# The second dense product of 14 token tiles as exchanged 64-row halves, first loads dealt to other queues, and a new table of steps

## The chip, the cores and the metric

One core of one Trainium2 chip. The metric is the device time of one execution in microseconds (us), as the median of several. The engines are named as the profile does: PE (TensorE matmuls), PEld (its weight loads), DVE (VectorE), ACT (ScalarE), POOL (GpSimd), SP (SyncE, which here only issues transfers). A q behind a name (SPq, ACTq) marks the queue from which a transfer is issued.

## The reference

One attention branch and one dense branch on the same normalized tokens, added to the input. 2048 tokens, width 448, 16 heads of 28, hidden width 1792; inputs and output in bfloat16. There is no gain or bias in the layer norm.

```python
xn = layernorm(x)                                  # over 448, eps 1e-5
q, k, v = split(xn @ wqkv)                         # 16 heads of 28
phi(t) = concat(softmax(t @ w_phi), softmax(-(t @ w_phi)))
kv = sum_s phi(k)_s v_s ;  z = sum_s phi(k)_s      # per head: 56 x 28, 56
o = (phi(q) @ kv) / (phi(q) @ z + 1e-6)
h = xn @ w1 + b1 ;  act = h * tanh(softplus(h))    # 2048 x 1792
out = x + o @ wo + act @ w2
```

## The kernel before

Tokens stand in 16 tiles of 128; two tiles are a unit (u = 0 to 7). A token tile is normalized (`ln_stats`, `ln_rstd`, `ln_apply`), and a unit's two normalized tiles are laid side by side (896 columns) and turned, into 7 chunks of 128 features by 128 tokens (`xnT`): 448 = 3.5 x 128, so the middle chunk holds 64 features of the one tile and 64 of the other. The turning is a transposing transfer of SP (step `xt{u}m`) or, at the start, seven PE transposes and two copies (`xt{u}E`, `xt{u}O`).

Products over 448 features are cut in passes (`passes`). Passes E and O take three chunks at the full height of 128 rows, for the even and the odd tile. Passes A, B and H take 64-row halves: two matmuls at a time, one on rows 0 to 63, one on rows 64 to 127, which write the two banks of a pair of PSUM banks, one for each tile of the unit. A gives the even tile the lower half and the odd tile the upper, B exchanges them, H is the shared middle chunk. So A + B + H = E + O + H. Before a pass A may write its banks, the pass B of the same pair must have ended and the other way round (`pe_pass`).

The query and key weights are first multiplied with w_phi, so that q and k leave PE already as q @ w_phi and k @ w_phi: Wk is turned by PE (`wtk`), Wq comes turned by four transposing transfers (`lqT0` to `lqT3`) and a DVE copy that doubles its last 64 columns (`qd`), and both are multiplied with a block-diagonal w_phi (`wmk`, `wmq`). ACT makes the exponentials of q and k (`exq`, `exk`), DVE the sums and POOL most of the normalizing of k (`kn`). When all eight `kv` steps are done, `kvz` and a transfer lay out kv and z, and per token tile `nd` makes numerators and denominators on PE and six DVE instructions make o, which a transfer turns (`ot`). The first dense product (`f0.*`, `f1.*`: 14 feature chunks for each half of the tokens, as passes A, B, H) ends in one ACT Mish activation per chunk. The second dense product is `g{t}`: for one token tile 14 matmuls of 128 rows by 448 columns. `wo{u}` is the output projection of a unit, as A, B, H, into the same bank as the second dense product of the tile; the last writer is followed by the DVE addition of x (`finish`), then the store.

A bank of a tile gets four parts (`PARTS = 4`: its g and wo A, B, H). The last tile of the order, 15, is written in two pieces (384 and 64 columns).

All instructions stand in the table ORDER: one list of step names. A step appends its instructions to the engines that it uses, so the order of the names is the order on each engine; waits are worked out from what a step reads and writes (`Program`). The ending of a name says who does it: s the SP queue, a ACT, d DVE, p POOL; in load steps it is the queue (`lkma` main rows of Wk on ACT's, `lps` w_phi on SP's). An engine takes its list strictly in order, and a waiting instruction holds all that stands behind it. At the start ACT's queue issues Wk, the tails (last 64 rows) of Wk and Wv, x tiles 4 and 5, 2 and 3, then Wv; SP's issues x tiles 6 and 7, w_phi, the four turned query weights, the rest of x and b1.

Lines of the profile: L300 load of x, L303 main rows of a weight, L308 tails, L312 turned Wq, L329 w_phi, L406 warm-up matmuls on zeros, L441 all passes of q, k, v and the first dense product, L514 PE transposes of tokens, L525 their transfer, L548 transposes of Wk, L572 weight products, L643 kv, L692 transpose of b1, L698 Mish, L721 nd, L790 finish, L825 second dense product, L842 output projection.

Of the kernel before, what the change touches and what calls it, by code (L numbers as in the profile page):

```python
# [12 lines left out]
D = 448  # L13
# [6 lines left out]
FC = F // P  # L20
# [118 lines left out]
class Banks:  # L139
# [44 lines left out]
xn1d q1B v4Aa e6 q1H k6H xt7m xn11d k6A v4Ba kn1.1p v6Ad kn2.0p k6B kn4.1p v6Hd xt0m q6A xt5m q6H l1ms v6Bd q6B k7H k7A k0B kn6.1p k7B k0H
kn1.0p k0A v5Aa kn6.0p v5Ha v7Aa k5A k5H v7Ha v5Ba k5B q4B v7Ba kn0.0p e2 e3 kn4.0p kn0.1p kn2.1p q4A f0.3B e13 e5 e4 q4H f0.2H f0.2A f0.3H
f0.0A f0.3A f0.0H v0Ad e12 kn7.0p kn7.1p v0Hd f0.2B v0Bd f0.0B kn3.1p q5H q5A kn5.1p los kn5.0d kn3.0d q0H q0A q5B kv6 kv4 kv0 kv2 kv1 q0B
f1.7A f1.7H f0.6H f0.6A f1.7B wob f1.12H f1.12A f0.6B f1.12B f0.9A kv5 kv3 kv7 f0.9H e9 kvz f0.13B f0.9B f1.11B f0.13A f1.11A f1.11H f0.10B
f0.13H f0.7B f0.10H f0.10A f1.10B l2.3a f0.12B f0.7A f0.7H f1.10H nd6 e8 f1.10A f0.12A f0.8H f0.12H f0.8A nd7 f1.0B e1 l2.1s e11 e0 f0.8B
f1.0H f1.0A q7B nd2 f1.2H q7A q7H f1.2B f1.8B f1.2A f1.8H f1.1H f1.8A f1.1A f0.11A f0.11H f1.1B l2.0s f1.6B f0.11B f1.6H nd4 f1.6A ot3m
f0.5A f1.9B e15 e10 e14 f0.5B nd5 l2.2s f0.4A f0.5H f1.9A f1.9H f0.4H f1.3A nd1 f1.3H f0.4B f1.5B f1.3B f0.1H nd0 f1.5H f0.1B f1.5A f0.1A  # L190
ot2m ot0m f1.4H f1.4A f1.13B f1.4B wo3A nd3 f1.13A wo3B nd8 wo3H f1.13H ot1m nd11 g6 g2 g7 wo0H nd13 wo0A nd14 wo1B wo0B nd10 wo1A wo1H g0
# [10 lines left out]
def _kernel(es, nc, A_x, A_wqkv, A_w_phi, A_wo, B_w1, B_b1, B_w2, out):  # L202
    def sb(name, shape, dtype):
        return es.enter_context(nc.sbuf_tensor(name, shape, dtype))
# [21 lines left out]
    W2 = sb("W2", [P, FC, D], BF16)  # L226
# [6 lines left out]
    actT = sb("actT", [P, FC, S], BF16)  # L233
# [46 lines left out]
    def bank(b, n=1):  # L280
        return PS[:, b * TCW:(b + n) * TCW]
# [57 lines left out]
    W2P = 4  # L339
# [76 lines left out]
    def pe(fn, r, w, tag, after=()):  # L416
        return op("PE", fn, r=r, w=w, tag=tag, after=after)
# [175 lines left out]
    def xchunk(c, par):  # L593
        return c if c == 3 or par == 0 else 4 + c
# [175 lines left out]
    LAST = int(ORDER.split()[-1][3:])  # L770

    def width(t):
        return CUT if t == LAST else D

    out_bank = {}
    PARTS = 4
    done = {t: 0 for t in range(NT)}

    def out_part(t):

        u = t // 2
        if u not in out_bank:
            out_bank[u] = take2()
        done[t] += 1
        return out_bank[u] + t % 2, done[t] == 1, done[t] == PARTS

    def finish(t):
        b = out_bank[t // 2] + t % 2
        n = width(t)
        op("DVE", lambda e: e.tensor_tensor(x_all[:, t, 0:n], bank(b)[:, 0:n], x_all[:, t, 0:n], ALU.add),  # L790
           r=[pb(b), ("x", t)], w=[("out", t)], tag=f"fin{t}")
        if t == LAST:
            last_columns(t, b ^ 1)
        if done[t] == done[t ^ 1] == PARTS:
            free2(out_bank[t // 2])

    def last_columns(t, b):
        assert done[t ^ 1] == PARTS
# [12 lines left out]
        op("DVE", lambda e: e.tensor_tensor(x_all[:, t, CUT:D], to, x_all[:, t, CUT:D], ALU.add), r=[pb(b), ("x", t)],  # L811
           w=[("outl", t)], tag=f"finl{t}")
# [7 lines left out]
    def ffn2(t):  # L820
        b, first, last = out_part(t)

        def f(e):
            for fc in range(FC):
                ins = e.matmul(bank(b)[:, 0:width(t)], actT[:, fc, tok(t)], W2[:, fc, 0:width(t)],  # L825
                               start=first and fc == 0, stop=last and fc == FC - 1)
# [34 lines left out]
    def add(name, fn, *args):  # L861
        steps[name] = lambda: fn(*args)
# [122 lines left out]
```

## Time and profile before

| | |
|---|---|
| median of 3 runs | 149.89 us (149.85 to 150.07) |
| profiled execution: time / span | 150.82 / 148.9 us |
| PE busy | 143.3 us, 96% |
| DVE, ACT, POOL busy | 101.0, 77.3, 33.2 us |
| granted clock of PE | 1.0 |
| HBM read / written | 7.02 / 1.84 MB |

The span runs from the first to the last instruction of the program; the time holds what lies around it too. A row of the timeline gives the start, the length, the engine, the line, the operation, the tiles as out<-in, rows by columns, and the number of instructions merged. Matmuls overlap, so a row's length is more than the distance to the next row's start; distances from start to start are what PE pays. `64*128` ahead of a shape means a half of 64 rows, `128*128` full height. In the chain of waits each row has its start, its length and who had the work.

### The profile page before, as it was taken

To read this page: it belongs to the slowest core of one execution; us is meant where nothing else is said; L and a number is where in the kernel's file an instruction comes from. 1 tells how busy PE (TensorE), PEld (TensorE's weight loads), DVE (VectorE), ACT (ScalarE), POOL (GpSimd) and SP (SyncE) were. 2 spreads that over 40 slices of the span, in tenths; PEclk is the share of its full clock that TensorE was granted. 3 is DMA by queue.
4 is the path that set the end of the run, shared out by engine and by line. 5 is a ranking of instruction groups with operands and counts; after the bars stand their busy time and mean duration, and the time that the engine had idled before them with its cause. 6 is when DMAs were issued, how large, how long until landed. Compare 5 with 4: busy or idle time off the path is not lost.

```text
span 148.9 us, 3768 instructions
## 1 busy us (share of the span) xinstructions
PE 143.3 (96%) x1628; PEld 74.6 (50%) x1628; DVE 101.0 (68%) x215; ACT 77.3 (52%) x90; POOL 33.2 (22%) x42
## 2 busy tenths in 40 slices
PE   7679999999999999999999999999999999999993
PEld 2355444555556454455444545545555555665552
DVE  0787998999989931089529996989997990042222
ACT  1596999999999986688995774100000000000000
POOL 4002435499999920000000000000000000000000
DMA  4999968999997003997383202200000347000115
GB/s 121 259 198 355 132 160 180 173 236 244 211 171 224 4 4 73 161 292 173 87 188 95 62 4 62 66 0 0 2 4 0 90 95 247 4 0 0 62 66 185
DMA packets 40980, 17.46 MB, mean 117 GB/s; under 512 B 34948, under 2 KB 40196, under 8 KB 40964
## 3 DMA queue, kind: packets, MB, share of 16 engines
q1 hardware_dynamic: 39044, 15.29, 44.6%
q10 hardware_dynamic: 1920, 1.93, 5.8%
q8 instruction: 13, 0.21, 0.7%
q14 instruction: 3, 0.02, 0.0%
HBM read 7.02 MB, written 1.84 MB: 60 GB/s over the span
## 4 chain that ended last, share of the span: by engine, by line
PE 91%; DMA 5%; ACTq 1%; DVE 1%; ACT 0%; issue 0%
PE PS L441 50%; PE PS L825 29%; PE PS L842 7%; DMA Wkv<-in_A_wqkv_dram 5%; PE PS L721 2%; PE PS L643 2%; ACTq L308 1%; PE PS L572 1%; ACTq L300 0%; DVE x_all L790 0%; ACTq L303 0%; ACT L357 0%; DVE x_all L811 0%; PE PS L692 0%
## 5 line engine op out<-in xcount | busy, mean ns | idle before, releaser
L441 PE MATMUL PS<-xnT,W 64*128 64x512 bf16 x392 | 45.0, 376 | 0.0
L825 PE MATMUL PS<-W,actT 128*128 128x448 bf16 (+1 forms) x224 | 42.7, 351 | 0.0
L698 ACT ACTIVATE actT<-PS,b1T 128x1024 bf16<-128x1024 f32 x28 | 29.8, 1114 | 8.7 <-PE PS L441 8.6
L825 PEld LDWEIGHTS PS<-W,actT 128*128 128x128 bf16 x224 | 21.6, 98 | 20.2 <-issue 0.7
L441 PEld LDWEIGHTS PS<-xnT,W 64*128 64x128 bf16 x392 | 18.5, 94 | 20.8 <-ACT actT L698 0.9
L625 POOL TENSOR_TENSOR actT<-actT,rSk 128x896 bf16<-128x896 bf16 x14 | 24.1, 1758 | 2.9 <-DVE rSk L623 2.9
L790 DVE TENSOR_TENSOR x_all<-PS,x_all 128x448 bf16<-128x448 f32 (+1 forms) x16 | 9.5, 616 | 19.7 <-PE PS L825 10.4
L621 DVE TENSOR_REDUCE Sk<-actT 128x32 f32<-128x896 bf16 x16 | 16.7, 1042 | 0.0
L613 ACT ACTIVATE actT<-PS 128x896 bf16<-128x896 f32 x16 | 13.7, 935 | 0.7 <-PE PS L441 0.7
L441 PE MATMUL PS<-Wkv,xnT 64*128 64x448 bf16 (+1 forms) x94 | 13.2, 350 | 0.8 <-DMA Wkv<-in_A_wqkv_dram 0.8
L441 PE MATMUL PS<-Wpq,xnT 64*128 64x448 bf16 (+1 forms) x106 | 13.2, 350 | 0.0
L441 PE MATMUL PS<-Wpk,xnT 64*128 64x448 bf16 (+1 forms) x100 | 12.7, 350 | 0.0
L480 DVE BATCH_NORM_STATS2 stats<-x_all 128x6 f32<-128x448 bf16 x16 | 9.7, 609 | 3.6 <-DMA x_all<-in_A_x_dram 3.6
L737 DVE COPY Sq<-PS 128x32 f32<-128x32 f32 x16 | 2.9, 184 | 13.5 <-PE PS L721 13.5
L746 DVE TENSOR_TENSOR v_all<-v_all 128x464 f32<-128x464 f32 x16 | 10.3, 642 | 0.6
L742 DVE TENSOR_TENSOR v_all<-PS,Sq 128x464 f32<-128x464 f32 x16 | 10.3, 641 | 0.6
L750 DVE TENSOR_TENSOR xn<-v_all,rden 128x448 bf16<-128x448 f32 x16 | 10.0, 624 | 0.6
L744 DVE TENSOR_TENSOR v_all<-PS,Sq 128x464 f32<-128x464 f32 x16 | 10.1, 629 | 0.0
L679 ACT ACTIVATE actT<-PS 128x896 bf16<-128x896 f32 x10 | 8.7, 941 | 0.0
L441 PEld LDWEIGHTS PS<-Wkv,xnT 64*128 64x128 bf16 (+1 forms) x94 | 5.4, 95 | 6.5 <-DMA Wkv<-in_A_wqkv_dram 1.0
L441 PEld LDWEIGHTS PS<-Wpq,xnT 64*128 64x128 bf16 (+1 forms) x106 | 5.4, 94 | 5.2 <-issue 0.4
L441 PEld LDWEIGHTS PS<-Wpk,xnT 64*128 64x128 bf16 (+1 forms) x100 | 5.3, 94 | 4.8 <-issue 0.2
(74 smaller groups left out, 117.1 us busy)
## 6 DMA issues: line engine op xcount, KB each, us to landing
out_dram<-x_all SPq DMA_DIRECT2D x7, 224.0 KB, 2.2
W<-in_B_w_dram SPq DMA_DIRECT2D x1, 1344.0 KB, 7.6
x_all<-in_A_x_dram SPq DMA_DIRECT2D x2, 448.0 KB, 4.6
Wkv<-in_A_wqkv_dram ACTq DMA_DIRECT2D x2, 336.0 KB, 5.8
Wo<-in_A_wo_dram SPq DMA_DIRECT2D x2, 336.0 KB, 3.8
W<-in_B_w_dram SPq DMA_DIRECT2D x2, 336.0 KB, 4.5
x_all<-in_A_x_dram SPq DMA_DIRECT2D x2, 224.0 KB, 3.2
x_all<-in_A_x_dram ACTq DMA_DIRECT2D x2, 224.0 KB, 5.4
```

The source lines that it names most:

```text
L441: ins = e.matmul(o, lhs(c, k), rhs(c, k), start=par in first and n == at[par][0], stop=par in last and n == at[par][-1])
L480: op("DVE", lambda e: e.bn_stats(stats[:, t, :], x_all[:, t, :]), r=[("x", t)], w=[("st", t)], tag=f"bn{t}")
L613: op("ACT", lambda e, s=s: e.activation(E_of(u)[:, s, :, :], two(b, D), ACT.Exp, scale=1.0 if s == 0 else -1.0), r=[pb(b), pb(b + 1)], w=[ ...
L621: op("DVE", lambda e: e.tensor_reduce(Sk[u][:, s, :], Eh(), AX.X, ALU.add), r=[("E", u, s)], w=[("Sk", u, s)], tag=f"Sk{u}.{s}")
L625: op(eng, lambda e: e.tensor_tensor(Eh(), Eh(), ap_on(rSk[u][:, s, 0:1], [[1, 2 * H], [0, DH]]), ALU.mult), r=[("E", u, s), ("rSk", u, s)] ...
L698: op("ACT", lambda e: e.activation(actT[:, fc, q * 1024:(q + 1) * 1024], bank(b, 2), ACT.Mish, bias=b1T[:, fc:fc + 1]), r=[("b1T",), pb(b) ...
L742: op("DVE", lambda e: e.tensor_tensor(tv(t1), num(0), sx(1), ALU.mult), r=[pb(b), pb(b + 1), ("Sq", i)], w=[("t1", i)], tag=f"ta{t}")
L744: op("DVE", lambda e: e.tensor_tensor(tv(t2), num(1), sx(0), ALU.mult), r=[pb(b), pb(b + 1), ("Sq", i)], w=[("t2", i)], tag=f"tb{t}")
L746: op("DVE", lambda e: e.tensor_tensor(t1, t1, t2, ALU.add), r=[("t1", i), ("t2", i)], w=[("t1", i)], tag=f"tc{t}")
L750: op("DVE", lambda e: e.tensor_tensor(o_sb[k][:, t % 2, :].rearrange("p (h d) -> p h d", d=DH), t1[:, :, 0:DH], ap_on(rden[i][:, 0:1], [[1 ...
L825: ins = e.matmul(bank(b)[:, 0:width(t)], actT[:, fc, tok(t)], W2[:, fc, 0:width(t)], start=first and fc == 0, stop=last and fc == FC - 1)
L842: ins = e.matmul(bank(b)[:, 0:w], oT_of(u)[lo:hi, cc * P:(cc + 1) * P], Wo[lo:hi, cc, 0:w], start=first and n == at[par][0], stop=last and ...
```

## The change

Three things change.

1. For tiles 0 to 13 `g{t}` is replaced by `gx{u}A` and `gx{u}B`: both tiles of a unit at once, in 64-row halves. A part takes the 14 chunks of the hidden width, two matmuls each: rows 0 to 63 for one tile, rows 64 to 127 for the other; part B exchanges them. A bank of these tiles then gets five parts. Tiles 14 and 15 keep g.
2. First loads: SP's queue now issues Wk first, then b1, w_phi, Wv, x tiles 12 to 15, three of the turned query weights, x 0 and 1, the last turned query weight, x 8 to 11. ACT's issues x tiles 4 and 5, 2 and 3, 6 and 7, then the tails. The memset of the block-diagonal w_phi goes from DVE to POOL.
3. ORDER is a new list. Among its differences: unit 2 instead of unit 3 is the first to be turned, and PE turns both units 2 and 3 (before: unit 3 by PE, unit 2 by a transfer); the full-height passes E and O stand for v2, k2, v3 instead of v1, v2, v3, k1, k3, q3; the statistics of tiles 5 and 6 are made by ACT; all copies of the query weight products are ACT's; DVE evacuates five of the eight v products (before two); 14 warm-up matmuls in one piece.

```diff
-    PARTS = 4
     done = {t: 0 for t in range(NT)}
+
+    def parts(t):
+        return 4 if t // 2 == LAST // 2 else 5
...
+    def ffn2_pair(u, part):
+        places = [out_part(2 * u + par) for par in range(2)]
+
+        def f(e):
+            for fc in range(FC):
+                for r in range(2):
+                    par, (lo, hi) = r ^ int(part == "B"), HALF[r]
+                    b, first, last = places[par]
+                    ins = e.matmul(bank(b)[:, 0:D], actT[lo:hi, fc, tok(2 * u + par)], W2[lo:hi, fc, 0:D],
+                                   start=first and fc == 0, stop=last and fc == FC - 1)
+            return ins
+        pe_pass(f, [("W2", i) for i in range(W2P)] + [("act", fc, u // 4) for fc in range(FC)], places[0][0], part,
+                f"gx{u}{part}")
+        for par, (b, first, last) in enumerate(places):
+            if last:
+                finish(2 * u + par)
...
-zero pwd lkma lx6.8s lkta lps pv lqT3 pi pe ph pp0 st7d lx4.6a z10 lqT0 pk table st6d lx2.4a lvma rs7a rs6a lqT1 lqT2 xn7d wtk0b xn6d wtk1a
+pi pe ph zero lx4.6a pp0 pwp pp2 lx2.4a table lx6.8a ep st4d z4 pv lkta st2d rs4p lkms st5a rs5p st6a lbs xn4d st7d lps rp6p lvms xn5d z10
```

PE's list at the start, behind the first warm-up matmuls, before (L548 turned Wk, L514 turned tokens, L572 weight products; Wkv with xnT are value products, Wpk and Wpq key and query products):

```order
L548 MATMUL PS<-ident,Wkv 112x128 x16
L514 MATMUL PS<-ident,xn 128x128 x7
L406 MATMUL PS<-zeros 128x512 x4
L572 MATMUL PS<-Wbd,Eq 128x112 x16
L441 MATMUL PS<-Wkv,xnT 128x448 x8
L572 MATMUL PS<-Wbd,WqT 128x112 x16
L441 MATMUL PS<-Wpk,xnT 128x448 x6
L692 MATMUL PS<-ident,b_rows 128x14
L441 MATMUL PS<-Wpk,xnT 128x448 x2
```

and now:

```order
L548 MATMUL PS<-ident,Wkv 112x128 x16
L692 MATMUL PS<-ident,b_rows 128x14
L514 MATMUL PS<-ident,xn 128x128 x7
L572 MATMUL PS<-Wbd,Eq 128x112 x16
L441 MATMUL PS<-Wkv,xnT 128x448 x5
L514 MATMUL PS<-ident,xn 128x128 x3
L441 MATMUL PS<-Wkv,xnT 128x448 x3
L441 MATMUL PS<-Wpk,xnT 128x448 x3
L514 MATMUL PS<-ident,xn 128x128 x4
L441 MATMUL PS<-Wpk,xnT 128x448 x3
L441 MATMUL PS<-Wkv,xnT 128x448 x3
L572 MATMUL PS<-Wbd,WqT 128x112 x16
```

The products of the turned query weights stand behind twice as many matmuls, a second unit is turned by PE, and b1 is turned ahead of all that.

SP's list at the start, before:

```order
L300 DMA x_all<-in_A_x_dram 128x896
L329 DMA Wbd<-in_A_w_phi_dram 28x4x28 x4
L312 DMA_TRANSPOSE WqT<-in_A_wqkv_dram 128x448 x4
L300 DMA x_all<-in_A_x_dram 128x1792
L337 DMA b_rows<-in_B_b_dram 14x128
```

and now:

```order
L303 DMA Wkv<-in_A_wqkv_dram 128x3x448
L337 DMA b_rows<-in_B_b_dram 14x128
L329 DMA Wbd<-in_A_w_phi_dram 28x4x28 x4
L303 DMA Wkv<-in_A_wqkv_dram 128x3x448
L300 DMA x_all<-in_A_x_dram 128x1792
L312 DMA_TRANSPOSE WqT<-in_A_wqkv_dram 128x448 x3
L300 DMA x_all<-in_A_x_dram 128x896
L312 DMA_TRANSPOSE WqT<-in_A_wqkv_dram 128x448
L300 DMA x_all<-in_A_x_dram 128x1792
```

Wk and Wv (the two rows L303) came onto this queue; the turned query weights moved behind Wv and four x tiles.

PE's list in the last third, before, from the tenth nd on (L721 nd, L825 the second dense product, L842 the output projection):

```order
L721 MATMUL PS<-KVZ,EqT 128x60 x16
L825 MATMUL PS<-W,actT 128x448 x42
L842 MATMUL PS<-Wo,Wkv 128x448 x2
L721 MATMUL PS<-KVZ,EqT 128x60 x16
L842 MATMUL PS<-Wo,Wkv 128x448 x6
L721 MATMUL PS<-KVZ,EqT 128x60 x16
L842 MATMUL PS<-Wo,Wkv 128x448 x12
L721 MATMUL PS<-KVZ,EqT 128x60 x16
L842 MATMUL PS<-Wo,Wkv 128x448 x8
L825 MATMUL PS<-W,actT 128x448 x42
```

and now, in the same third (numbers of the changed file: L842 the halves of the second dense product, L861 the output projection):

```order
L842 MATMUL PS<-W,actT 128x448 x28
L861 MATMUL PS<-Wo,Wkv 128x448 x2
L721 MATMUL PS<-KVZ,EqT 128x60 x16
L842 MATMUL PS<-W,actT 128x448 x56
L861 MATMUL PS<-Wo,Wkv 128x448 x10
L721 MATMUL PS<-KVZ,EqT 128x60 x16
L842 MATMUL PS<-W,actT 128x448 x28
L721 MATMUL PS<-KVZ,EqT 128x60 x16
L861 MATMUL PS<-Wo,Wkv 128x448 x8
L842 MATMUL PS<-W,actT 128x448 x56
```

The full-height runs of 42, 42 and 70 matmuls between halves became runs of 28 or 56 halves. The rows give the size of the result, not how many rows of the array are used.

More of the change, by code (lines that the diff above doesn't have):

```diff
@@ L184 @@
[L184 to L191, printed above, removed]
@@ L192 @@
-g3 g1 wo2B nd12 wo2H nd15 wo2A ot6m ot5m ot7m nd9 g5 g4 g13 g12 ot4m g10 wo4A wo5H wo7A wo6H wo4B wo5A wo7H wo6B wo5B wo7B wo4H wo6A sto1 g8
-g9 g11 sto2 g14 sto0 sto4 sto5 stt14 sto3 g15 sto6 stt15
+pi pe ph zero lx4.6a pp0 pwp pp2 lx2.4a table lx6.8a ep st4d z4 pv lkta st2d rs4p lkms st5a rs5p st6a lbs xn4d st7d lps rp6p lvms xn5d z10
+wtk0b lx12.16s wtk1b lqT1 b1 lqT3 lqT2 xt2Od xt2Ea wmk0a wmk1a v2Ha v2Oa xn7d xn6d st3d xt3Ea st15d lx0.2s lqT0 rp2p v2Ea k2O st14d xn2d qd
+rp14a xt3Oa xn14a k2E pp1 xn3d v3Ed xn15d lx8.12s wmq1a st12d wmq0a v3Od st8d st9d xt7m k2H rp8p xt1m st13d v3Hd xn9d l1ts k3H k3A q2B k3B
@@ new lines @@
+xn8d st0d q2A xt4m rp12p q3A xn13d q3H xn12d st1d st11d v7Hd q2H v7Ad q3B xt6m q1A v7Bd l1ms q1H k1B q1B k1A k1H v1Aa k7H k7A rp0p v1Ba xn0d
+xn1d st10d rp10p kn1.0p v6Bd v1Ha k7B v6Ad xn10a kn3.1p k4B v6Hd k6A k4H k4A k6H xt0m v4Aa xn11d v4Ha k6B kn2.0d k0A e2 kn4.1p v4Ba e7 e6
+k0B e3 q6A k0H e5 xt5m e4 kn7.1p kn2.1p q6H q4A q6B f0.3A e13 q4B f0.3H kn6.0p kn1.1p v0Bd q4H f0.3B v0Ad f0.0A v0Hd f0.0H f0.2A f0.2H f0.0B
+f0.2B q0B k5A kn6.1p kn4.0p v5Bd k5B q5A k5H q5H v5Ad kn0.1p v5Hd kn3.0p q5B q0A kn5.1p kv2 kv6 kv4 kv1 e12 q0H f0.12H f0.12A f1.12B f0.12B
@@ new lines @@
+kn5.0d f1.0A los f1.0H f1.12H f1.12A f1.0B f1.10A f1.10H e9 f0.10B pk f1.10B f0.10H l2.3s e10 kn0.0p f0.10A f1.11A wob f1.7H f1.11H kn7.0d
+kv3 kv5 kv0 kv7 f0.8B f1.7B e0 kvz f0.8A f0.8H f0.1H f1.7A f1.11B f0.7A f0.7H f0.1A f0.13H f0.13A nd0 e1 e8 e11 f0.7B f0.13B f0.1B f1.8B nd4
+f1.8A f1.8H q7A f0.9B q7H nd3 q7B f1.2A f0.9A f1.2B l2.2a f0.11B f1.2H f0.5H f0.5A f0.9H f0.11A f0.5B f0.11H f1.6H f1.6A f1.9A f1.6B f1.9B
+l2.0a f1.5A f1.9H f1.5H nd1 f0.4H f1.5B f0.4A f0.6B f1.13H nd5 f0.6A e15 l2.1a e14 f0.6H f0.4B f1.13A f1.1A nd2 f1.13B f1.1H f1.3H f1.3A
@@ L194 @@
+f1.1B f1.3B nd6 gx1B nd7 ot2m ot1m ot0m nd10 gx1A f1.4B gx2B f1.4A wo1B ot3m wo2B nd11 gx2A f1.4H wo3A wo1A wo2A nd13 gx3A wo1H nd14 gx3B
+gx0A wo0H wo3B wo2H nd9 gx0B nd8 wo0A wo3H gx4A ot5m sto1 gx5B ot4m wo5B wo0B nd12 gx4B ot6m nd15 wo4B gx5A sto0 ot7m wo5A gx6B wo6B wo5H
+wo4A gx6A wo7A wo6H wo4H wo7B wo6A wo7H sto6 sto3 sto2 g14 stt14 g15 sto5 sto4 stt15
 """
@@ L784, in out_part @@
         done[t] += 1
-        return out_bank[u] + t % 2, done[t] == 1, done[t] == PARTS
+        return out_bank[u] + t % 2, done[t] == 1, done[t] == parts(t)
     def finish(t):
@@ L793, in finish @@
             last_columns(t, b ^ 1)
-        if done[t] == done[t ^ 1] == PARTS:
+        if done[t] == done[t ^ 1] == parts(t):
             free2(out_bank[t // 2])
     def last_columns(t, b):
-        assert done[t ^ 1] == PARTS
+        assert done[t ^ 1] == parts(t)
         to = bank(b)[:, D:D + 64]
@@ L889, in _kernel @@
             add(f"wo{u}{part}", wo, u, part)
+        for part in "AB":
+            add(f"gx{u}{part}", ffn2_pair, u, part)
         for s in range(2):
```

3 lines of the change are left out of this document (removed).

## The prediction

> **What bounds the kernel now.** TensorE (PE) is busy 96% of the span, so I read its waits first, then the chain that ended last, then its busy time by stage, then its timeline.
>
> ```profile
> PE PS L548 <- DMA Wkv<-in_A_wqkv_dram: 1.4, 2, 1.2
> ...
> PE PS L441 <- DMA Wkv<-in_A_wqkv_dram: 0.8, 1, 0.8
> ```
> ```profile
> 3.55 7.24 DMA Wkv<-in_A_wqkv_dram
> ...
> 10.84 1.31 PE PS L441 x6
> 12.15 0.96 PE PS L572 x16
> ...
> 145.92 0.56 DVE x_all L790
> ```
> PE's waits are all at the start (the one left out is for the first memset). From 10.84, when the value weights (Wv) land, to 145.9 it is the chain. So the time is: when PE's unbroken stretch begins, plus what is in it, plus 3 us behind it. Removing anyone else's work gains nothing; delaying it can only cost, and there the margin is thin in one stage:
>
> ```profile
> 14.37:54.93 40.56, 40.56 (x618) 20.84 (x619) 36.80 (x77) 39.67 (x46) 30.23 (x27) 1.00 0.79 164
> 54.93:92.50 37.57, 37.57 (x499) 18.18 (x490) 22.56 (x48) 27.91 (x29) 0.00 (x0) 1.00 0.52 119
> ```
> Behind the stretch and its length stand the busy times of PE, its weight loads, VectorE (DVE), ScalarE (ACT) and GpSimd, then the clock. PE runs without a gap at full clock while ACT is busy 39.67 of 40.56 us.
>
> **The new form of the second dense product.** Does a pair of 64-row halves run as fast as one 128-row matmul, and what does a change of form cost? PE's timeline has both (L825 the dense product, L842 the output projection in halves, L721 in halves too):
>
> ```profile
> 92.23 0.38 PE L721 MATMUL PS<-KVZ,EqT 64*128 64x60 bf16 x16
> 92.55 8.12 PE L825 MATMUL PS<-W,actT 128*128 128x448 bf16 x42
> 100.60 0.36 PE L842 MATMUL PS<-Wo,Wkv 64*128 64x448 bf16 x2
> ...
> 101.81 1.30 PE L842 MATMUL PS<-Wo,Wkv 64*128 64x448 bf16 x12
> 102.94 0.38 PE L721 MATMUL PS<-KVZ,EqT 64*128 64x60 bf16 x16
> 103.16 0.92 PE L842 MATMUL PS<-Wo,Wkv 64*128 64x448 bf16 x8
> ...
> 114.17 13.42 PE L825 MATMUL PS<-W,actT 128*128 128x448 bf16 x70
> 127.52 0.93 PE L842 MATMUL PS<-Wo,WqT 64*128 64x448 bf16 x8
> ```
> From start to next start: 42 full matmuls 8.05, 70 take 13.35. The 28 more cost 5.30, so 0.189 each, and 8.05 - 42 x 0.189 leaves 0.10 us at the change to halves. Twelve halves take 1.13, so 0.188 a pair: the same. The change into full height costs as much: the 16 of L721 take 0.32 ahead of L825, 0.22 elsewhere. So the 14 tiles themselves cost what they did, and what goes is the changes of form: three runs of L825 lie between halves, 6 changes. The last run (tiles 14, 15) keeps its one.
>
> The weight loads leave little room, though:
>
> ```profile
> L825 PEld LDWEIGHTS PS<-W,actT x224: 95/98/99, 92.5 to 145.4; 128*128 128x128 bf16 x112
> L842 PEld LDWEIGHTS PS<-Wo,Wkv x56: 92/94/95, 89.4 to 113.5; 64*128 64x128 bf16 x56
> ```
> Two half loads of 94 ns fill the 189 of a pair. I take the pair at 0.189, as L842 has it with loads of the same size; if loads from the activations stayed at 98, a pair would take 0.196, and 196 pairs +1.4 us.
>
> A rule speaks against this edit too: the Trainium skill, TensorEngine Tiling (Array Packing), Instruction Overhead, gives each matmul about 60 cycles of overhead. The halves are 196 matmuls more, and a column takes 0.42 ns here (448 in 0.189 us), so by that page they would cost an estimated 4.9 us. The rows disagree (0.188 a pair against 0.189), so I add nothing. The same page's Key Properties say that a change of tiling mode drains the engine; the trace agrees, at 0.10 us each.
>
> The new order also has fewer changes of form at the start, where before shows them:
>
> ```profile
> 7.53 0.55 PE L514 MATMUL PS<-ident,xn 128*128 128x128 bf16 x7
> 7.92 1.03 PE L406 MATMUL PS<-zeros 128*128 128x512 bf16 x4
> ...
> 12.95 1.30 PE L441 MATMUL PS<-Wpk,xnT 128*128 128x448 bf16 x6
> 14.18 0.18 PE L692 MATMUL PS<-ident,b_rows 14*128 14x14 bf16 x1
> 14.29 0.36 PE L441 MATMUL PS<-Wpk,xnT 64*128 64x448 bf16 x2
> 14.58 1.60 PE L441 MATMUL PS<-Wpq,xnT 128*128 128x448 bf16 x8
> ```
> Six full matmuls at 12.95 take 1.23 (1.13 + 0.10), the bias turn 0.11, the halves behind it 0.29 (0.19 + 0.10). Counting changes in both orders from the first matmul that needs Wv: 17 before, 6 after. Eleven at 0.106 (exit 0.095 and about 0.01 on the next start) are **-1.17 us**. Unit 2 is now turned by PE instead of a DMA: 7 turns, 0.39 in the rows (7.53 to 7.92): **+0.39**. All other matmuls stay.
>
> **The start.** Wv moves from the end of ACT's first loads to SP's queue, behind Wk, the bias rows and the four w_phi loads, which wait for a memset that moves to GpSimd. The query weights (WqT, four transposing loads) now stand behind Wv and x tiles 12 to 15, the last behind two tiles more.
>
> ```profile
> 1.18 1.95 SPq L329 DMA_DIRECT2D Wbd<-in_A_w_phi_dram  x4
> 3.18 5.11 SPq L312 DMA_TRANSPOSE WqT<-in_A_wqkv_dram  x4
> 8.97 0.41 SPq L337 DMA_DIRECT2D b_rows<-in_B_b_dram  x1
> 1.95 0.20 POOL L385 MEMSET Eq<- 128x128 uint32 x1
> ```
> ```profile
> Wo<-in_A_wo_dram SPq DMA_DIRECT2D x2, 336.0 KB, 3.8
> xnT<-xn SPq DMA_TRANSPOSE x7, 2.8
> WqT<-in_A_wqkv_dram SPq DMA_TRANSPOSE x4, 6.1
> ```
> GpSimd ended its padding of Eq at 2.15; in the new order the memset for w_phi stands behind that padding and one of the same size has left the place ahead of it: 2.2. SP's issues by these rows: w_phi 2.2 to 4.2, Wv at 4.25, x at 4.75, three WqT from 5.4 at 1.3 each, x at 9.25, the last WqT at 9.7. Wv of 336 KB lands 3.8 later as the equal Wo did (8.0) or 7.2 later as it did itself (the chain's row; 11.5). I take 4.5: its queue is ahead of the transposes, which shared its stretch before.
>
> By then another chain decides. Tiles 4 and 5 are loaded first; tile 5's three statistics run on ACT, its inverse root on GpSimd. The first row is from the view of the loads of x (L300), the second of the warm-up:
>
> ```profile
> DMA to landing us min/median/max: 3.0/4.6/5.6
> ...
> 0.88 4.10 PE L406 MATMUL PS<-zeros 128*128 128x512 bf16 x10 [0.88 <-POOL zeros L363]
> ```
> ```profile
> 12.93 0.22 POOL L486 TENSOR_SCALAR lnv<-mv 128x2 f32<-128x2 f32 x1 [10.31 <-DVE mv L481]
> 13.24 0.71 POOL L488 TENSOR_TENSOR rstd<-lnv,mhalf 128x2 f32<-128x2 f32 x1
> 17.90 1.05 ACT L504 ACTIVATE xn<-x_all,shift,rstd 128x64 bf16<-128x64 bf16 x2
> ```
> My estimate: x at 0.74 + 3.2 = 3.9, +1.8 for three dependent ACT operations (448 elements are split over the last row's two), then two roots in a row (1.0 each) to 7.15, +0.6 normalizing, +0.4 turns, +0.8 copies on DVE, +0.3 first halves: the first matmul on Wv at **9.5** against 10.84, **-1.3**. Bounds: -1.8 if x lands earlier, +0.7 if Wv needs 7.2. The 14 warm-up matmuls cost nothing while that chain covers them: zeros come 0.9 later, and ten took 4.1 (half clock at first), so 14 end near 6.6.
>
> **The query weights.** PE then has 15 full matmuls and 7 turns (15 x 0.189 + 0.39 = 3.2) before the products of WqT: ready at 12.7. DVE must first copy a strip of WqT:
>
> The first row is from the view of WqT's loads (L312), the second from DVE's timeline:
>
> ```profile
> DMA to landing us min/median/max: 4.8/6.1/7.7
> ...
> 11.87 0.23 DVE L316 COPY WqT<-WqT 128x256 bf16<-128x256 bf16 x1 [0.90 <-DMA WqT<-in_A_wqkv_dram]
> ```
> Before, PE lost 0.17 here (six matmuls from 10.84 end at 11.97, the product starts at 12.15): that goes, **-0.17**. Now the last WqT lands at 9.7 + 2.8 = 12.5 (like a turn of xn) or 9.7 + 4.8 to 7.7 = 14.5 to 17.4 (as itself). Those four queued behind w_phi and ran beside Wv, which is gone by 9 now; I take 3.0, so 12.7, and 13.0 with copy and signal: **+0.3**, bounds 0 and +5.0. Behind the copy on DVE stand tiles 3 and 15, for two turning DMAs of SP (2.8 each); the values of unit 7 need the first some 5 us later. That fits.
>
> **ScalarE behind it.**
>
> ```profile
> 14.69 1.73 ACT L613 ACTIVATE actT<-PS 128x896 bf16<-128x896 f32 x2 [0.57 <-PE PS L441]
> 16.30 1.73 ACT L679 ACTIVATE Eq<-PS 128x896 bf16<-128x896 f32 x2
> ```
> An exponential takes 0.80 from start to start. ACT now makes all four copies of the query products (two were DVE's), two normalizations for one, and six statistics; it hands three value copies of 0.8 to DVE. Up to the first Mish it has 24 us of work (12 pairs of 1.6, four copies of 0.44, two of 0.8, two normalizations of 0.66) and PE comes to the last of these banks 25.4 after the query products (the new order's pairs at 0.189 for 448 columns, so 0.216 for 512): just in time, and at eight places with 0.1 to 0.3 to spare. I put **+0.3**, bounds 0 and +0.8. DVE takes the three copies and drops two statistics and two copies, so it stays even. From 55 us on DVE (22.56 of 37.57) and ACT (27.91) have room, and by the same count the last load of W2 is issued near 80 and needed near 87.
>
> **Sum.** -1.3 - 1.17 + 0.39 - 0.17 + 0.3 + 0.3 = -1.65 against the profiled execution, whose span is 148.9 and time 150.82. The median is 149.89; 1.92 and about 1.0 lie around the span. The tail behind PE stays. So span 147.2 and median 149.89 - 1.65 = **148.2 us**.
>
> **Rivals.**
> - *Only the changes of form pay.* Wv or tile 5 comes as late as Wv before: PE begins at 10.84 and the query weights are covered: -1.17 + 0.39 - 0.17 = -0.95, 148.9 us. For it: Wv's own 7.2. Against: its stretch no longer holds the transposes. 0.17. The Trainium skill, DMA: Bandwidth & Descriptors, Issuing engines are not separate DMA queues, speaks for it: DMAs of all queues share 16 engines, and another issuer saves only issue time; no row here decides it.
> - *Late query weights (slower).* The last WqT needs as long from issue as before. With no other stall the gain without the wait, 1.95, is used up when the product starts at 12.7 + 1.95 = 14.65, so when the load needs over 4.7 us; at its own median of 6.1 the product starts at 16.1 and the kernel takes 151.3. For it: its own minimum was 4.8. Against: what was in its way. 0.11.
> - *ACT becomes the bound* in 14 to 55 us: each of eight places late by 0.2 us gives back 1.6: 149.8 us, no change. 0.07.
> - *Weight loads bind the halves* (98 ns, above): +1.4, 149.6 us, no change. For it: the margin of 1 ns. Against: 64-row loads take 94 wherever they stand. 0.02.
> - The page's 60 cycles a matmul: +4.9, 153.1 us; 0.01, as the rows of pairs bear it out so little.
>
> **Chances and range.** My forecast has 0.62, its own range 147.4 to 148.7. Range for all: 147.4 to 149.9, which takes in the first and third rival. A measurement of this kernel can tell about 0.2% (0.3 us) from no change: faster 0.62 + 0.17 = 0.79; same 0.07 + 0.02 = 0.09; slower 0.11 + 0.01 = 0.12.
>
> **What would show it.** The first matmul on Wv near 9.5; the products of WqT near 13.0, with a wait on the DVE copy of 0.3; no wait of PE above 0.3 behind that; one change of form from 56 us on; halves of the dense product at 0.189 a pair. Wrong would be: that copy ending after 14.5, waits of PE on ACT that sum to over 1 us, or over 0.195 a pair.

## The result, and the profile after

The changed kernel takes 150.79 us (median of five, 150.32 to 151.31) against 149.89 for the kernel before: a ratio of 1.0054, 95% interval 1.0028 to 1.0079, so slower by 0.5%. I had predicted 148.2 us and a range of 147.4 to 149.9. Its profiled execution has a span of 148.7 us (time 150.90), with the clock granted in full.

Up to 29 us it runs nearly as forecast, with the first product of the value weights 0.3 us later. TensorE's (PE) timeline at its start, with the start and length of each group in us:

```profile
7.97 0.56 PE L514 MATMUL PS<-ident,xn 128*128 128x128 bf16 x7
8.55 1.05 PE L572 MATMUL PS<-Wbd,Eq 112*128 112x112 bf16 x16
9.53 1.04 PE L441 MATMUL PS<-Wkv,xnT 64*128 64x448 bf16 x5
...
13.07 0.95 PE L572 MATMUL PS<-Wbd,WqT 112*128 112x112 bf16 x16
```

Two halves start at 9.53. With their change of form they take 0.30 (0.29 for the two at 14.29 before), so the first product of the value weights' main rows starts at 9.83. The products of the query weights start at 13.07, and PE came to them without a wait. The halves of the second dense product run as forecast too; the next rows are from PE's timeline and from the groups of weight loads:

```profile
95.81 2.81 PE L842 MATMUL PS<-W,actT 64*128 64x448 bf16 x28
98.45 0.81 PE L441 MATMUL PS<-xnT,W 64*128 64x512 bf16 x6
```
```profile
L842 PEld LDWEIGHTS PS<-W,actT 64*128 64x128 bf16 x392 | 18.6, 94 | 16.7
```

Fourteen pairs take 98.45 - 95.81 = 2.64 us, 0.189 a pair, and their weight loads 94 ns.

What is new stands in PE's waits:

```profile
PE PS L406 <- POOL zeros L363: 1.7, 1, 1.7
PE PS L441 <- DMA xnT<-xn: 1.4, 1, 1.4
PE PS L548 <- DMA Wkv<-in_A_wqkv_dram: 0.5, 1, 0.5
```

The first and the third are ahead of the first product. The second is in the middle of the stretch that was to have no wait. The chain of work that ended last runs through it, here with start and length of each piece, and PE's timeline shows the place:

```profile
22.69 0.89 DVE xn L508 x3
23.61 8.13 DMA xnT<-xn
31.87 15.68 PE PS L441 x158
```
```profile
29.75 0.73 PE L441 MATMUL PS<-Wpk,xnT 64*128 64x448 bf16 x6
31.87 0.74 PE L441 MATMUL PS<-Wpk,xnT 64*128 64x448 bf16 x6 [1.38 <-DMA xnT<-xn]
```

Six halves take 0.57 from start to start, so 31.87 - 29.75 - 0.57 = 1.55 us are lost ahead of the keys of unit 0. They need the turned x of unit 0 (L525, `xt0m` in the order), whose transfer took 8.13 us; the seven of the kernel before took 2.8 in the median. What stood ahead of it is on SP's queue:

```profile
18.82 2.75 SPq L525 DMA_TRANSPOSE xnT<-xn  x2
21.61 0.58 SPq L303 DMA_DIRECT2D W<-in_B_w_dram  x1
23.61 1.33 SPq L525 DMA_TRANSPOSE xnT<-xn  x1
24.98 3.49 SPq L687 DMA_TRANSPOSE EqT<-actT  x1
28.50 4.26 SPq L687 DMA_TRANSPOSE EqT<-Eq  x2
```

At 21.61 the main rows of W1 are issued (L303, `l1ms`), 1344 KB that land 7.8 us later, at 29.4. The new order has `xt6m l1ms xt0m`. In the kernel before the same queue had the load of W1 behind the turn of unit 0:

```profile
24.57 4.05 SPq L525 DMA_TRANSPOSE xnT<-xn  x3
28.66 0.58 SPq L303 DMA_DIRECT2D W<-in_B_w_dram  x1
29.29 6.94 SPq L687 DMA_TRANSPOSE EqT<-actT  x2
```

The turns behind it there were of features (`EqT`), which PE first uses in L721 at 63 us, and PE waited for none of them.

That wait explains 1.55 us, and the miss is 2.6. Most of the rest is in what I subtracted from, as the first experiment shows.

### The profile page after: what moved, and what is told of

It reads as the page before. It is cut to its first block, busy times and chain, and to the rows that moved or that the text cites. A ratio compares the mean times of both kernels' runs of the same rounds, so it can differ in the third digit from the quotient of the medians.

```text
span 148.7 us, 4210 instructions
## 1 busy us (share of the span) xinstructions
PE 142.7 (96%) x1849; PEld 75.6 (51%) x1849; DVE 104.5 (70%) x215; ACT 78.1 (53%) x96; POOL 32.6 (22%) x46
## 4 chain that ended last, share of the span: by engine, by line
PE 77%; DVE 9%; DMA 9%; ACT 1%; issue 1%; POOL 1%; ACTq 1%; DVEq 0%
PE PS L441 37%; PE PS L842 25%; PE PS L861 7%; DMA xnT<-xn 5%; DVE stats L480 4%; PE PS L827 3%; DMA x_all<-in_A_x_dram 3%; DVE xn L508 3%; PE PS L721 2%; PE PS L643 2%; DVE mv L481 1%; DVE v_all L521 1%; ACTq L300 1%; POOL rstd L488 0%; ACT junk L472 0%
## 5 line engine op out<-in xcount | busy, mean ns | idle before, releaser
L698 ACT ACTIVATE actT<-PS,b1T 128x1024 bf16<-128x1024 f32 x28 | 29.6, 1112 | 18.9 <-PE PS L441 18.9
L842 PE MATMUL PS<-W,actT 64*128 64x448 bf16 x392 | 39.0, 349 | 0.0
L441 PEld LDWEIGHTS PS<-xnT,W 64*128 64x128 bf16 x392 | 19.5, 94 | 20.6 <-issue 1.0
L842 PEld LDWEIGHTS PS<-W,actT 64*128 64x128 bf16 x392 | 18.6, 94 | 16.7
L625 POOL TENSOR_TENSOR actT<-actT,rSk 128x896 bf16<-128x896 bf16 x13 | 21.7, 1695 | 8.9 <-DVE rSk L623 7.8
L792 DVE TENSOR_TENSOR x_all<-PS,x_all 128x448 bf16<-128x448 f32 (+1 forms) x16 | 9.2, 615 | 14.1 <-PE PS L861 10.7
L441 PE MATMUL PS<-Wpk,xnT 64*128 64x448 bf16 (+1 forms) x106 | 13.6, 350 | 1.4 <-DMA xnT<-xn 1.4
L441 PE MATMUL PS<-Wkv,xnT 64*128 64x448 bf16 (+1 forms) x100 | 13.9, 350 | 0.0
L441 PE MATMUL PS<-Wpq,xnT 64*128 64x448 bf16 x112 | 13.7, 350 | 0.0
L480 DVE BATCH_NORM_STATS2 stats<-x_all 128x6 f32<-128x448 bf16 x14 | 8.6, 611 | 2.7 <-DMA x_all<-in_A_x_dram 2.7
L441 PEld LDWEIGHTS PS<-Wpq,xnT 64*128 64x128 bf16 x112 | 5.5, 94 | 5.0 <-ACT Wpq L519 0.4
```

What stands on the lines that cost most here:

```text
L441: ins = e.matmul(o, lhs(c, k), rhs(c, k), start=par in first and n == at[par][0], stop=par in last and n == at[par][-1])
L480: op("DVE", lambda e: e.bn_stats(stats[:, t, :], x_all[:, t, :]), r=[("x", t)], w=[("st", t)], tag=f"bn{t}")
L625: op(eng, lambda e: e.tensor_tensor(Eh(), Eh(), ap_on(rSk[u][:, s, 0:1], [[1, 2 * H], [0, DH]]), ALU.mult), r=[("E", u, s), ("rSk", u, s)] ...
L698: op("ACT", lambda e: e.activation(actT[:, fc, q * 1024:(q + 1) * 1024], bank(b, 2), ACT.Mish, bias=b1T[:, fc:fc + 1]), r=[("b1T",), pb(b) ...
L842: ins = e.matmul(bank(b)[:, 0:D], actT[lo:hi, fc, tok(2 * u + par)], W2[lo:hi, fc, 0:D], start=first and fc == 0, stop=last and fc == FC - 1)
```

## The experiments

The theory after the two traces: (1) the transfer of unit 0 is held by W1; (2) the profiled execution of before was slower than its usual ones, because its value weights landed late, and so the gain at the start isn't there; (3) halves and changes of form do what the prediction says. The rivals are with each run.

### The kernel before, once more

No edit.

> The kernel before, unchanged. Theory (the profiled execution of before, 150.82 us, was not a typical one): spans near 148.0 for times near 149.9, and in the new profile the stretch of TensorE begins earlier than 10.84 us, near 9.9, with the same length behind it (10.84 to 145.72, 134.9 us). Rival (a profiled execution is as fast inside, and what lies around the span varies): span 148.9 again, the value weights landing near 10.8 again, and the time alone lower.

Measured: 149.97 us (149.54 to 150.56), beside 149.84 for the runs of before that it shares with the next kernels; ratio 1.0012, 0.9996 to 1.0028. The spans of these 39 executions go from 147.4 to 148.5, with a median near 148.0. The 148.9 on which my sum stood is above them all (of 40 later ones, on two other chips, a single one was longer, 149.5). The kernel before starts differently from one execution to the next, as the chain shows in this profile and in those of two other runs whose edits leave its first 90 us alone (halves alone, and halves in another order; in this sequence):

```profile
3.57 6.67 DMA Wkv<-in_A_wqkv_dram
...
10.28 1.31 PE PS L441 x6
```
```profile
3.56 6.24 DMA Wkv<-in_A_wqkv_dram
...
9.84 1.31 PE PS L441 x6
```
```profile
3.67 6.14 DMA Wkv<-in_A_wqkv_dram
...
9.86 1.31 PE PS L441 x6
```

The same load of 336 KB took 6.1 to 6.7 us, and 7.24 in the profile I read. PE starts 0.05 behind it each time. From that start to the last columns (L804) the two profiles of the unchanged kernel take the same: 145.72 - 10.84 = 134.88 and 145.16 - 10.28 = 134.88. So the kernel before varies in its start, by some 1 us, and if a late start is paid in full its usual start is an estimated 10.84 - (148.9 - 148.0) = 9.94. That is good to some 0.2: in the two profiles that start at 9.84 and 9.86 the stretch up to 54 us is 0.3 and 0.1 longer, in small holes between 15 and 20 us, so the earliest starts aren't kept whole. The changed kernel starts at 9.83, and at 9.72 to 10.06 in the seven other profiles with its loads: there its value weights land by 8.8 and no longer set the start. The gain at the start is near 0.1 us and not 1.3. Part (2) holds. The time around the span, the rival, was 1.9 in the profiled execution and 1.9 in the mean of the rest.

### W1 behind the turn of unit 0

```diff
-... xt6m q1A v7Bd l1ms q1H ... xt0m v4Aa xn11d ...
+... xt6m q1A v7Bd q1H ... xt0m l1ms v4Aa xn11d ...
```

> The changed kernel with one transfer moved: the load of W1's main rows (1344 KB) is issued behind the turning transfer of unit 0 instead of ahead of it. Theory (the turn of unit 0 waits in SP's queue for W1): it lands some 2.8 us behind its issue at 23.6 and TensorE's 1.56 us wait at the keys of unit 0 goes: 150.8 - 1.55 = 149.2 us. W1 would land near 24.9 + 7.8 = 32.7, ahead of the first product that needs it (35.65 - 1.55 = 34.1). Rival 1 (the wait only moves, to W1 or to a bank that ScalarE or VectorE frees): 150.5 to 150.8 us with a wait of over 1 us at another place between 30 and 45 us. Rival 2 (the wait costs nothing at the end, something later sets it): 150.8 us.

Measured: 149.39 us (149.12 to 150.22) against 149.84, ratio 0.9975, 0.9956 to 0.9994. The profile has one wait of PE left, ahead of everything, and the next rows are its SP queue and its transfers between 23 and 25.2 us (KB and us to landing):

```profile
PE PS L406 <- POOL zeros L363: 1.6, 1, 1.6
```
```profile
20.23 4.48 SPq L525 DMA_TRANSPOSE xnT<-xn  x2
24.75 0.59 SPq L303 DMA_DIRECT2D W<-in_B_w_dram  x1
25.39 2.44 SPq L687 DMA_TRANSPOSE EqT<-actT  x1
```
```profile
W<-in_B_w_dram SPq DMA_DIRECT2D x1, 1344.0 KB, 6.5
xnT<-xn SPq DMA_TRANSPOSE x1, 4.3
```

The wait of 1.55 is gone, and the time fell by 1.4 us from that of the changed kernel (in another set of runs, where the kernel before took 149.84 and not 149.89). Unit 0 still took 4.3 and not 2.8; W1 was issued 1.3 us behind it and ran beside it, which is the likely reason. It landed at 27.8 and was needed at 30.3. W1 landed at 31.3 and its first product ran at 34.0 without a wait. Rivals 1 and 2 fall. Two of the twelve executions, though, had spans of 148.0 and 148.2, where the others had 147.1 to 147.7.

### W1 from ScalarE's queue

Is unit 0 held by its place in SP's queue, or by W1's bytes, whoever issues them? In the first of two runs ScalarE issues the load at the place in the order where SP did:

```diff
-... xt6m q1A v7Bd l1ms q1H k1B q1B k1A ...
+... xt6m q1A v7Bd l1ma q1H k1B q1B k1A ...
```

> The changed kernel with W1's main rows issued at the same place of the order by ScalarE's queue instead of SP's. Theory A (the turn of unit 0 is held by its place in SP's queue): it lands some 2.8 us behind its issue, no wait at the keys of unit 0, 149.2 us plus at most the 0.6 us that ScalarE needs for the issue. Theory B (it is held by the 1344 KB on the shared DMA engines, whoever issues them): it still lands near 31.7 when issued near 23.6, the wait of 1.5 us stays, 150.8 us or a little more.

Measured: 152.8 us in the profiled execution, with the clock granted in full; three more took 154.4 to 156.9 at a granted clock of 0.978 to 0.989. It is slower on any reading (ratio 1.0277, 1.0225 to 1.0329), and slower than either theory said. ScalarE comes to that place earlier than SP does, at 20.09, 0.35 us ahead of the turn of unit 6. So it was unit 6 that came late: W1 landed at 26.6, the turn of unit 6 at 28.2, 7.8 us behind its issue, and PE waited until then, longer than expected:

```profile
PE PS L441 <- DMA xnT<-xn: 3.2, 1, 3.2
```

A turn on SP's queue had been held by a load on ScalarE's, which speaks for theory B, but at another unit than foreseen. The second run has it one pair of exponentials later:

```diff
-... xt6m q1A v7Bd l1ms q1H k1B q1B k1A ...
+... xt6m q1A v7Bd q1H k1B q1B l1ma k1A ...
```

> The changed kernel with W1's main rows issued by ScalarE's queue, one pair of exponentials later than in the first run of that kind, so near 22 us, between the turns of units 6 and 0. Theory A (place in SP's queue holds unit 0's turn): the turn of unit 0, issued near 23.5, lands within 4.5 us, as it did with W1 behind it, and TensorE doesn't wait. Theory B (the 1344 KB hold any turning transfer issued behind them, from whichever queue): it lands at 29.5 or later, some 1 to 2 us behind W1, and TensorE waits 0.5 to 2 us at the keys of unit 0.

Measured: 150.69 us, ratio 1.0036, 1.0010 to 1.0062. ScalarE's timeline, the transfers between 22 and 24 us, and PE's wait:

```profile
22.20 0.39 ACTq L303 DMA_DIRECT2D W<-in_B_w_dram  x1
```
```profile
W<-in_B_w_dram ACTq DMA_DIRECT2D x1, 1344.0 KB, 7.4
xnT<-xn SPq DMA_TRANSPOSE x1, 8.3
```
```profile
PE PS L441 <- DMA xnT<-xn: 1.8, 1, 1.8
```

The turn of unit 0 was the next thing on SP's queue, 1.5 us behind W1 and on another queue, and took as long as behind it on the same one. Theory A falls. The Trainium skill, DMA: Bandwidth & Descriptors, Issuing engines are not separate DMA queues, says that DMAs of all issuers run on the same 16 engines and that another issuer saves only issue time; this pair of rows agrees with it.

### The halves alone, in the order before

```diff
-... nd11 g6 g2 g7 wo0H nd13 wo0A nd14 wo1B ... wo1H g0 g3 g1 wo2B ...
+... nd11 gx3A gx1A gx3B wo0H nd13 wo0A nd14 wo1B ... wo1H gx0A gx1B gx0B wo2B ...
-... nd9 g5 g4 g13 g12 ot4m g10 wo4A ... sto1 g8 g9 g11 sto2 g14 ...
+... nd9 gx2A gx2B gx6A gx6B ot4m gx5A wo4A ... sto1 gx4A gx4B gx5B sto2 g14 ...
```

> The kernel before, with its own loads and order, and only the second dense product of tiles 0 to 13 as exchanged 64-row halves (part A of a unit where its first tile stood, part B where its second stood). Theory (halves cost 0.189 a pair and what goes is 6 changes of form at 0.106 us): 149.89 - 0.64 = 149.25 us. Rival 1 (the halves gain nothing, or their weight loads bind): 149.9 us, or up to 151.3 at 0.196 a pair. Rival 2 (tiles finish later, since both are done with the second part): a wait of TensorE for a bank behind 93 us, 149.5 to 150 us.

Measured: 150.58 us (149.78 to 151.04) against 149.84, ratio 1.0037, 1.0017 to 1.0057: slower by 0.7 us, where 0.64 was to be gained. In PE's timeline, with its idle time in brackets:

```profile
101.13 0.39 PE L721 MATMUL PS<-KVZ,EqT 64*128 64x60 bf16 x16 [0.28 <-DVE x_all L792]
...
113.42 8.77 PE L842 MATMUL PS<-W,actT 64*128 64x448 bf16 x86
```

Two new losses. Unit 3 is now finished with its second part, so both of its additions on DVE (L792) come together, at 99.9, and the next L721 of PE waits behind them: 0.44 from start to start. And `gx2A gx2B` and `gx6A gx6B` stand directly behind each other: the last row is cut at 122, and up to there 86 halves take 8.77 us, where at 0.0946 each they would take 8.13. From start to start, part B follows a part A of its own unit 0.23, 0.23 and 0.25 us late at the three such places. The last half of A and the first of B go to the same bank, and the program has B's first wait for the end of A (`pe_pass`). Together that is -0.64 + 0.44 + 0.71, and the 0.3 of early holes named above, which makes +0.8; its stretch from the first product to the last columns is 0.85 longer than before, so little is left over. The next run takes the parts of a unit apart:

```diff
-... wo0A nd14 wo1B wo0B ... gx2A gx2B gx6A gx6B ... gx4A gx4B gx5B ...
+... wo0A wo1B nd14 wo0B ... gx2A gx6A gx2B gx6B ... gx4A gx5B gx4B ...
```

> The kernel before with halves as in the run of halves alone, but no unit's part B directly behind its part A (three places: gx2A gx6A gx2B gx6B for gx2A gx2B gx6A gx6B, and gx4A gx5B gx4B for gx4A gx4B gx5B), and the den product nd14 one step later, behind wo1B. Theory (the 150.58 us of the run of halves alone came from those places: about 0.23 us where the last half of A and the first of B go to the same bank, three times, and 0.44 at nd14, against a gain of 0.64): 150.58 - 0.69 - 0.44 = 149.45 us, or 149.87 - 0.64 = 149.2 us counted from the kernel before. Rival (halves are slower in themselves): 150.2 us or more.

Measured: 149.63 us (149.18 to 150.28) against 150.03, ratio 0.9966, 0.9943 to 0.9988.

```profile
102.24 0.39 PE L721 MATMUL PS<-KVZ,EqT 64*128 64x60 bf16 x16 [0.24 <-DVE v_all L744]
...
113.18 9.05 PE L842 MATMUL PS<-W,actT 64*128 64x448 bf16 x94
```

Here, cut at 122 as well, 94 halves take 9.05, which is 0.48 less by their count (9.05 - 8 x 0.0946 = 8.29 against 8.77): two pauses of 0.24 are gone. The wait behind unit 3 isn't, though I had expected that; it moved one step on with DVE (0.40 from start to start). So 0.64 is gained and 0.40 lost, which makes 0.24, and 0.4 is measured between the medians (0.2 to 0.9 by the interval). The halves are as fast as full matmuls; in that order they need other places around them.

### Full height again in the new order

```diff
-... nd6 gx1B nd7 ... nd10 gx1A f1.4B gx2B f1.4A wo1B ...
+... nd6 g3 nd7 ... nd10 g2 f1.4B g5 f1.4A wo1B ...
```

(with W1 behind unit 0, and so for all fourteen tiles.)

> The changed kernel with W1 behind unit 0's turn, and the second dense product of tiles 0 to 13 back in full 128-row matmuls at the places of the halves (part A's place: the first tile of the unit, part B's: the second). In this order the tiles stand singly between halves, so it has 30 changes of form behind the first product of the value weights instead of 6. Theory (halves at 0.189 a pair, 0.106 us a change): 149.4 + 24 x 0.106 = 151.9 us. Rival 1 (the halves themselves are slower than a full matmul, and part of the gain of fewer changes went there): well under 151.9, at 150.5 or less. Rival 2 (the form does not matter): 149.4 us.

Measured: 151.74 us against 150.03, ratio 1.0109, 1.0062 to 1.0156, where the theory said 151.9. Its timeline of PE, and then that of the same stretch with halves (the run with W1 behind unit 0):

```profile
87.60 0.38 PE L721 MATMUL PS<-KVZ,EqT 64*128 64x60 bf16 x16
87.91 2.82 PE L827 MATMUL PS<-W,actT 128*128 128x448 bf16 x14
90.67 0.61 PE L721 MATMUL PS<-KVZ,EqT 64*128 64x60 bf16 x32
```
```profile
87.58 0.38 PE L721 MATMUL PS<-KVZ,EqT 64*128 64x60 bf16 x16
87.80 2.81 PE L842 MATMUL PS<-W,actT 64*128 64x448 bf16 x28
90.45 0.60 PE L721 MATMUL PS<-KVZ,EqT 64*128 64x60 bf16 x32
```

From the first of these rows to the last it is 3.07 against 2.87: 0.20 for two changes of form. Over the whole stretch, from the first product of the value weights to the last columns, it is 136.67 against 134.09: 2.58 for 24 changes, 0.107 each. Both rivals fall: the order of the changed kernel rests on the halves.

### Ten warm-up matmuls

```diff
-pi pe ph zero lx4.6a pp0 pwp pp2 ... ep st4d z4 pv lkta ...
+pi pe ph zero lx4.6a pp0 pwp pp2 ... ep st4d pv lkta ...
```

> The changed kernel with W1 behind unit 0's turn and without the first four warm-up matmuls (ten are left, as before). In the profile with fourteen TensorE ran without a gap from 1.65 to its first product of the value weights at 9.85. Theory 1 (another chain decides the start: tile 5's statistics, root and turns): first product at 9.7 to 9.9 again, 149.4 us. Theory 2 (the warm-ups are the chain): first product up to 1 us earlier, 148.4 to 149.0 us. Theory 3 (fewer warm-ups leave the clock low for longer): first product later than 10.0, 149.6 us or more.

Measured: 150.75 us (149.61 to 151.15) against 150.03, ratio 1.0039, 1.0013 to 1.0066. The first product of the value weights stands at 9.90, so the start is as theory 1 has it. The time is 1.3 us longer than that theory said, and for another reason. PE's waits, ScalarE's timeline and the transfers from 24.5 to 28 us:

```profile
PE PS L441 <- ACT Eq L679: 0.6, 1, 0.6
PE PS L441 <- ACT actT L679: 0.4, 1, 0.4
```
```profile
36.43 1.73 ACT L679 ACTIVATE Eq<-PS 128x896 bf16<-128x896 f32 x2 [1.66 <-DMA EqT<-Eq]
```
```profile
W<-in_B_w_dram SPq DMA_DIRECT2D x1, 1344.0 KB, 8.5
...
EqT<-actT SPq DMA_TRANSPOSE x1, 8.7
EqT<-Eq SPq DMA_TRANSPOSE x1, 7.1
```

Unit 0's turn took 2.7 us here, so W1 didn't hold it, but W1 took 8.5 us and not 6.5, the turns of features behind it came late, ScalarE may not write over their strips until they have left, and PE waited for ScalarE. W1 moved whole fits, then, with hardly any margin. Two of the twelve spans were 147.5 and 147.6, ten 148.4 to 149.1. The chip alone isn't the reason: the run at full height was on this chip too, issues the same loads in the same order with fourteen warm-ups, and there W1 took 6.7 us and the four spans lie within 0.3. With fourteen warm-ups and W1 behind unit 0, two spans in 22 were long (both in the first run of that kind), with ten warm-ups ten in 12. So the long executions go with fewer warm-ups, but no trace shows how these could slow W1: it is issued at 24.8 in both.

### W1 in three pieces

```diff
+def load_w1(c, eng):                     # rows c * 128 to c * 128 + 127
+    dma(eng, lambda e: e.dma_start(W1[:, c, :], B_w1[c * P:(c + 1) * P, :]), ...)
...
-... v7Bd l1ms q1H ... xt0m v4Aa ... e2 kn4.1p v4Ba e7 e6 k0B ...
+... v7Bd l1c0s q1H ... xt0m l1c1s v4Aa ... e2 kn4.1p v4Ba e7 l1c2s e6 k0B ...
```

> The changed kernel with W1's main rows in three transfers of 448 KB instead of one of 1344 KB: the first where the one stood, the second behind the turn of unit 0, the third behind the turns of the second features' first two strips. Theory (a bulk transfer holds the turning transfers issued behind it for as long as its bytes take): each piece holds them for some 2.5 us instead of 6.5 to 8.5; unit 0's turn lands by 28.5 (needed near 30.3), the four turns that ScalarE's exponentials of units 4 and 6 need by 34, W1 by 33 (needed at 34.0). TensorE has no wait over 0.3 us behind its first product in any execution, so spans stay at the fast end of those with W1 moved whole (147.1 to 147.5) and the time is 149.1 to 149.4 us. Rival (the pieces only spread the delay, and a turn is late again): spans over 148, 150 us or more.

> The kernel with W1 moved whole behind unit 0's turn once more, on the chip of the run in pieces. Theory (W1 takes 6.5 to 8.5 us from one execution to the next, and when it is slow the turns behind it reach ScalarE late, as in the run with ten warm-ups): spans in two groups, near 147.3 and near 148.4, with a median time of 149.4 to 150.5 us depending on how many fall in each. Rival (the late turns came from leaving out the warm-ups): one group near 147.3, 149.4 us.

Measured: in pieces 149.04 us (148.88 to 149.11) against 149.94, ratio 0.9936, 0.9923 to 0.9950, with all six spans between 147.1 and 147.3. Moved whole, on the same chip: 149.29 us (148.87 to 149.57), ratio 0.9952, 0.9936 to 0.9968, spans 146.8 to 147.5. In pieces PE has no wait behind its first product. Its transfers between 21.5 and 24 us, the first piece and two turns:

```profile
W<-in_B_w_dram SPq DMA_DIRECT2D x1, 448.0 KB, 3.7
xnT<-xn SPq DMA_TRANSPOSE x2, 3.7
```

Unit 0's turn landed at 28.35 and the last piece of W1 at 33.0, as expected. The version in pieces is 0.9 us faster than the kernel before and 1.75 faster than the changed one (measured in another set of runs), and its executions lie closest together. Against W1 moved whole it isn't shown to gain: the spans have medians of 147.1 and 147.2, and most of the 0.25 us between the times lies around the span (1.9 and 2.1), for a reason that no trace shows. The two groups of spans that I expected of W1 moved whole did not show on this chip; it came out as the rival said, one group and 149.3 us. So the theory that W1 varies by itself from one execution to the next isn't confirmed, and the rival, that the late turns came from leaving out the warm-ups, fits these runs better except for the two long executions of the first run with W1 moved.

## Why the prediction was wrong, by its own steps

- **The sum was made against one execution.** "Span 147.2 and median 149.89 - 1.65": the terms were read from an execution with a span of 148.9 and then taken from the median, whose spans are near 148.0. The 0.9 between them sat in one term, the landing of the value weights, so the gain on just that term was not there to be had in the median. I had the hint in the numbers: time 150.82 in the profile, 149.89 in the median, and 1.92 and about 1.0 "around the span", which I took for a difference outside it.
- **The start, -1.3.** The changed kernel starts at 9.83 where I put 9.5, and before usually at 9.94 where I put 10.84. So -0.1, within some 0.2. The mechanism was right (the value weights land 4.0 us behind an issue at 4.13 and no longer decide), its size was not. The sum for 9.5 has a slip too: from 7.15 its own terms (0.6, 0.4, 0.8 and 0.3) come to 9.25. GpSimd ended the root of tile 5 at 7.09, as forecast, and from there to the first product it took 2.74 us; the turns start at 7.97 and 16 weight products stand between them and the first halves (8.55 to 9.53). What decides now lies within some tenths: the tails of the weights, for which PE waits up to 7.28, tile 5's turns at 7.97, and in other executions PE's own warm-ups.
- **The missing term: a moved bulk load.** Of SP's queue I followed the loads of the start and the turns of units 1 and 7, and of the weights only W2. That the main rows of W1 now stand ahead of the turn of unit 0 was in the order and had a row in the trace: 1344 KB behind which two turns took 6.94 us to issue. It cost 1.55, and "no wait of PE above 0.3 behind that" fell with it.
- **Changes of form, -1.17, and the turns, +0.39:** right. From the first product to the last columns 134.88 before, 135.74 after; without the wait 134.2, and 134.1 and 134.2 in the runs without it. That is -0.7 to -0.8, where these terms and the old wait (-0.17) make -0.95. The full height run measured 0.107 a change. In the run of halves in another order the same stretch is 134.74, 0.14 shorter than before, where the six changes (-0.64), the wait behind unit 3 (+0.40) and the early holes (+0.1) make the same.
- **The halves at 0.189 a pair:** right, with loads of 94 ns, so that rival falls. The 60 cycles a matmul (the Trainium skill, TensorEngine Tiling (Array Packing), Instruction Overhead) were not added to the halves: 14 pairs took 2.64 us, the time of 14 full matmuls, where my estimate from the page's figure had 4.9 us more for the 196 extra matmuls.
- **The query weights, +0.3:** no wait at all. The products stood at 13.07 for a forecast of 13.0, but PE itself came there only at 13.07, and the last query weights had landed at 12.5. *Late query weights*, the slower rival to which I gave 0.11, did not happen; the kernel was slower for another late transfer.
- **ScalarE just in time, +0.3:** two holes of 0.09 and 0.11 us, at 15.7 and 54.2 from start to start. About 0.2, so this rival falls as well.

Together: -0.1 at the start, -0.75 behind it, +1.55 at unit 0, and about +0.2 around the span (2.1 in the mean of the five executions after, 1.9 before; the reason stays open) make +0.9, which is what was measured. With W1 moved whole the change is worth 0.45 to 0.65 us less time than before, and 0.9 less with W1 in pieces. So two steps failed, the size of the start and the missing term of W1; the changes of form and the halves held for the reasons that were given.

## What to carry to other kernels

When an order of work changes, list for every bulk load the small transfers that are issued within its landing time, on any queue, and who waits for them; a load that is moved by a few places can cost more than all the rest of the change brings. Here it was enough to put it behind the small transfer that is needed first, or, in pieces, most of it. Before a term is taken from a profile, compare its span with the spans of other executions: if one late landing makes the difference, a gain on that landing isn't a gain on the median. Removing changes of form pays what is counted, if the parts of one pair don't follow each other directly and nothing waits for tiles that are finished later.

## What was not expected of the hardware

A turning transfer behind a bulk load doesn't land with it but later: 1.0 us in the kernel before (36.3 and 37.3), 2.3 after the change (29.4 and 31.7), 2.4 with the load on ScalarE's queue (29.6 and 32.0). In the runs with W1 whole behind unit 0 it is 0.9 to 1.0, for a turn of features issued 0.6 behind W1. In the changed kernel the DMA engines moved almost nothing in between. Its throughput between 19 and 31 us, in 40 slices of 0.3 us:

```profile
GB/s 119 299 323 215 300 221 207 175 161 276 289 282 108 131 36 131 167 358 370 406 358 287 382 311 275 227 323 306 351 256 163 108 38 104 178 1 2 8 10 108
```

From 29.5 to 30.7 it is 1 to 10 GB/s, with unit 0's turn and one of features issued and a third in issue. Why they start so late, the runs don't show. Nor do they show why the same load of 336 KB at the start of the kernel before takes 6.1 us in one execution and 7.2 in another.
